# A recurrent-attention and gated-feed-forward kernel: the weights' guard made a later check, and the state-times-q products put on four 64x64 tiles

## The chip, the cores and the metric

The kernel runs on one core of a Trainium2 chip. The metric is device microseconds (us) of one execution. The core has five engines with instruction queues of their own: TensorE (PE, matmuls into PSUM; PEld is its weight load), VectorE (DVE), ScalarE (ACT), GpSimd (POOL) and SyncE (SP), which here issues every DMA. Each engine takes its instructions strictly in the order in which the program lists them.

## The reference

For each of 4 batches and 8 heads, a 48x48 state is decayed row by row with a sigmoid gate, gets the outer product of k and v added, and is read by q; the heads' outputs, side by side, are the input x of a gated feed-forward part that mixes each token with the one before it.

```python
f = 1.0 / (1.0 + np.exp(-f_logit))                 # (4, 8, 768, 48)
for t in range(S):
    state = f[:, :, t, :, None] * state + np.einsum('bhd,bhe->bhde', k[:, :, t], v[:, :, t])
    y[:, :, t] = np.einsum('bhd,bhde->bhe', q[:, :, t], state)
...
xk = mu_k * x + (1.0 - mu_k) * x_prev              # x: (4, 768, 384)
xr = mu_r * x + (1.0 - mu_r) * x_prev
k = np.maximum(xk @ w_k, 0.0)                      # w_k: 384 x 1024
v = k * k @ w_v                                    # w_v: 1024 x 384
r = 1.0 / (1.0 + np.exp(-(xr @ w_r)))              # w_r: 384 x 384
return (r * v).astype(np.float32)
```

The three weights arrive as 64-bit floats and are converted on the chip.

## The kernel before

**Attention in chunks.** Time is cut into 24 chunks `i` of 128 tokens (6 for each batch; `cs` is the chunk's place in its batch). Heads go in four pairs `j`; the head `g2` of a pair lies on partitions 0 to 47 or 64 to 111. For a chunk, `b` is the running product of the gates (a scan, L203), `bl` its last column, `ln`/`rb` give 1/b on ACT, and q and k are scaled with them (L213, L221 to L233). On PE, `SC` makes the 128x128 scores in small tiles (L274), `TR` transposes k (L259, copied out as `ktk`, L262), `ZQ` multiplies the state `z` with q (L284), `VV` adds scores times v to the same sums (L284), and `PP` makes the chunk's own contribution to the state (L315) in the PSUM tile `pp`. The masks `ma`, `mb` (L300) take the scores out of PSUM. `zs` and `z` (L247, L249) add the old state to `pp` and gate it; they come before the next chunk's `ZQ`. `y` (L330) copies the sums out of the PSUM tile `py`, negated, into `x` (pairs 0 to 2) and `stage` (pair 3). `y` of a chunk comes before `ZQ` and `VV` of the next, as there is one `py`.

**Feed-forward in units.** Three chunks make a unit `u` of 384 tokens; there are 8. When the three `y` are done, six small DMAs (`spread`, L385) move the fourth pair's rows from `stage` into the free rows of `x`. The mix (`d`, L395; `xm`, L404; `xh`, L412 or L413; `xl`, L419) makes six operands, each split into a high and a low part, because each product is made as three matmuls, high by high, high by low and low by high (`mm3`, L427). PE then runs `F` (8 groups of 9 matmuls with w_k), `R` (3 groups of 9 with w_r) and `W` (6 groups of 12 with w_v). ACT and DVE square what `F` gives (L450 to L459), POOL subtracts the high part (L465), `sg` applies the sigmoid, and `o` (L517) multiplies and is stored.

**Weights.** A 64-bit word is made into a float by `add_words`, in 18 pieces: 8 of w_k, 4 of w_r, 6 of w_v. For a piece, ACT takes the absolute value of the high half (`A`, L543), DVE clamps it from below at 2 to the power of -15 (`M`, L546, the guard for weights too small for the cheap conversion), shifts (`S`, L548), merges the low half's top bits (`T`, L551) and the sign and exponent (`X`, L554); ACT then rounds to the high part (`H`, L557) and POOL makes the low part (`L`, L561). The words of the last four pieces of w_v take turns in two buffers, `words`, which a piece leaves free when its `L` is done.

**What sets the order.** A planner (`Plan.schedule`) lists every step with a place, the engines that can do it and a cost for each, and simulates: it takes the step that can start first, and by place between equals. Its order is fixed on each engine. The constants at the file's head (`LEAD`, `PREP`, `WORDS`, `DEAR`) and the costs in `pl.add` steer it and do no work themselves. `F{u}.{f}` needs the `L` of w_k's piece f in the first unit, `R` all of w_r, a first half of `W` three pieces of w_v.

**An unusual path.** If the smallest `bl` is under a bound, a flag makes all engines run `general`, a slow exact version, at the end. The inputs here do not raise it.

Of the kernel before, what the change touches and what calls it, by code (L numbers as in the profile page):

```python
# [47 lines left out]


class Plan:  # L50
# [104 lines left out]
class Rwkv:  # L155


    def __init__(self, nc=None, tc=None):
# [17 lines left out]
    def add_attention(self, pl, i):  # L176
# [104 lines left out]
        first = [None, None]  # L281

        def ymm(g2, j, lhs, rhs, stop):
            m = nc.tensor.matmul(  # L284
                self.py[64 * g2 : 64 * g2 + lhs.shape[1], j], lhs, rhs, start=first[g2] is None, stop=stop,
                skip_group_check=True,
            )
# [36 lines left out]
        def y_out(e):  # L324

            for r in (slice(0, D), slice(64, 64 + D)) if cs == 0 else (slice(0, P),):
                for o, i_ in ((self.b("x", u)[r, :, 1 + t0 : 1 + t0 + C], self.py[r, 0:3]),
                              (self.b("stage", u)[r, t0 : t0 + C], self.py[r, 3])):
                    if e is nc.scalar:
                        e.activation(o, i_, AF.Copy, scale=-1.0)  # L330
# [50 lines left out]
    def spread(self, x, stage, j):  # L381

        for g2 in (0, 1):
            r = 64 * g2
            self.nc.sync.dma_start(x[r + 48 : r + 64, j, 1:], stage[r + 16 * j : r + 16 * j + 16, :])  # L385

    def add_mix(self, pl, u, k0, dst, alone=False):
# [46 lines left out]
        for f in range(NF):  # L434
# [36 lines left out]
        for t in range(UC):  # L471
# [343 lines left out]
```

## Time and profile before

| | |
|---|---|
| median of 3 runs | 392.2 us (391.81 to 392.32) |
| the profiled execution | 392.84 us; its span, first to last instruction, 391.1 us |
| mean granted TensorE clock | 0.977 |
| busy, share of the span | PE 87%, DVE 59%, ACT 61%, POOL 47% |
| moved by DMA | 34.17 MB, 87 GB/s over the span |

The span is 1.7 us shorter than the execution's time. Times in the trace count from the span's start. A row of the timeline gives start, length, engine, line, operation, output and inputs, count, and in brackets the idle time before it and what ended it. In a grouped row stand the count, the busy sum in us and the mean in ns, then the idle time ahead of the group. PE writes each fp32 matmul of the program as two records.

### The profile page before, as it was taken

How to read it: one execution, taken by the hardware profiler on the slowest of the kernel's cores; microseconds unless marked ns; L12 is line 12 of the kernel's file. 1: busy time of each engine (PE TensorE's matmuls, PEld its weight loads, DVE VectorE, ACT ScalarE, POOL GpSimd, SP SyncE). 2: the span in 40 equal slices, each digit the busy share in tenths (PEclk: the TensorE clock that was granted, in tenths of full speed). 3: DMA queues.
4: the chain of work that ended last, by engine and by line, in shares of the span. 5: the costliest groups of instructions: out<-in, count | busy, mean ns of one | idle time of the engine just before them, and what ended most of it. 6: DMA issues, size and time to landing. Idle time of an engine off the chain costs nothing.

```text
span 391.1 us, 8274 instructions
## 1 busy us (share of the span) xinstructions
PE 339.2 (87%) x3241; PEld 314.9 (81%) x3241; DVE 231.2 (59%) x429; ACT 237.1 (61%) x458; POOL 184.6 (47%) x212
## 2 busy tenths in 40 slices
PE   0077227699999999999999999999999999999994
PEld 0066126689898998999899989999899989999993
DVE  6989699998797588318851688049822731161001
ACT  4773348868478765747675655856584436565830
POOL 1451377764667564534574364618361613334600
PEclk9999859999999999999999999999999999999999
DMA  7999611343550243421321123032301100011001
GB/s 250 402 372 233 150 54 55 108 99 84 140 118 5 59 99 108 117 60 38 103 62 33 45 83 102 2 75 76 91 20 30 47 23 2 1 37 40 3 21 47
DMA packets 17918, 34.17 MB, mean 87 GB/s; under 512 B 2928, under 2 KB 13040, under 8 KB 17872
## 3 DMA queue, kind: packets, MB, share of 16 engines
q1 hardware_dynamic: 17872, 33.57, 30.1%
q8 instruction: 27, 0.44, 0.5%
q14 instruction: 19, 0.16, 0.1%
HBM read 27.66 MB, written 4.72 MB: 83 GB/s over the span
## 4 chain that ended last, share of the span: by engine, by line
PE 78%; DVE 9%; DMA 8%; ACT 1%; issue 1%; SPq 1%; DVEq 0%
PE pm L427 59%; PE py L284 10%; PE pss L274 5%; DMA v<-in_vt 3%; PE pm L259 2%; DMA f<-in_zt 2%; DMA x<-stage 2%; PE pp L315 2%; DVE pm L548 1%; DVE pm L551 1%; DVE pm L546 1%; DVE xm L404 1%; DVE pm L395 1%; DMA x<-in_wr 1%; DVE words L554 1%
## 5 line engine op out<-in xcount | busy, mean ns | idle before, releaser
L427 PE MATMUL pm<-xh,wk 128*128 128x384 f32 x384 | 107.5, 350 | 19.1 <-DVE words_k2h L554 13.5
L427 PE MATMUL pm<-wv,k2h 128*128 128x384 f32 x384 | 99.8, 341 | 0.4 <-DVE xm L404 0.4
L465 POOL TENSOR_TENSOR k2l<-kk,k2h 128x384 fp32r<-128x384 f32 x64 | 65.0, 1018 | 60.3 <-ACT kk L459 38.3
L427 PEld LDWEIGHTS pm<-xh,wk 128*128 128x128 f32 x384 | 71.6, 192 | 22.8 <-issue 14.1
L419 POOL TENSOR_TENSOR xl<-xm,xh 128x384 fp32r<-128x384 f32 x48 | 53.3, 1125 | 50.3 <-DVE xh L413 39.7
L427 PEld LDWEIGHTS pm<-wv,k2h 128*128 128x128 f32 x384 | 69.0, 188 | 1.8 <-issue 0.9
L427 PE MATMUL pm<-xl,wk 128*128 128x384 f32 x192 | 65.9, 343 | 0.0
L427 PE MATMUL pm<-wv,k2l 128*128 128x384 f32 x192 | 64.8, 338 | 0.0
L300 DVE TENSOR_TENSOR ss<-pss,cst_sb 128x512 f32<-128x512 f32 x48 | 30.8, 683 | 53.5 <-PE pss L274 53.3
L450 ACT ACTIVATE r<-pm 128x384 f32<-128x384 f32 x64 | 31.4, 490 | 32.2 <-PE pm L427 27.9
L274 PE MATMUL pss<-qk 64*64 64x128 f32 (+1 forms) x768 | 23.1, 258 | 22.1 <-DVE qk L225 22.1
L274 PEld LDWEIGHTS pss<-qk 64*64 64x64 f32 x768 | 19.6, 139 | 27.4 <-DVE qk L225 22.1
L427 PE MATMUL pm<-wr,xh 128*128 128x384 f32 x144 | 38.5, 349 | 0.0
L427 PEld LDWEIGHTS pm<-xl,wk 128*128 128x128 f32 x192 | 36.8, 192 | 0.0
L395 DVE TENSOR_TENSOR pm<-x 128x384 f32<-128x384 f32 x24 | 18.2, 757 | 30.9 <-DMA x<-stage 30.7
L427 PEld LDWEIGHTS pm<-wv,k2l 128*128 128x128 f32 x192 | 36.1, 188 | 0.0
L455 ACT ACTIVATE k2h<-r 128x384 fp32r<-128x384 f32 x64 | 33.6, 525 | 2.0
L517 DVE TENSOR_TENSOR o<-pm,lg 128x384 f32<-128x384 f32 x24 | 13.2, 551 | 35.7 <-PE pm L427 35.7
L221 POOL TENSOR_TENSOR qk<-qk,rb 128x256 f32<-128x256 f32 x24 | 22.5, 937 | 24.5 <-ACT rb L211 14.2
L203 DVE TENSOR_TENSOR_SCAN pm<-f,low 128x512 f32<-128x512 f32 x24 | 32.8, 1365 | 0.0
L412 ACT CAST xh<-xm 128x384 fp32r<-128x384 f32 x36 | 18.2, 514 | 20.2 <-DVE xm L404 20.0
L459 ACT ACTIVATE kk<-r 128x384 f32<-128x384 f32 x59 | 30.0, 509 | 0.1
(81 smaller groups left out, 529.2 us busy)
## 6 DMA issues: line engine op xcount, KB each, us to landing
qk<-in_qkt SPq DMA_DIRECT2D x40, 192.0 KB, 3.4
v<-in_vt SPq DMA_DIRECT2D x24, 192.0 KB, 2.5
out<-o SPq DMA_DIRECT2D x24, 192.0 KB, 1.9
words<-in_wv SPq DMA_DIRECT2D x6, 512.0 KB, 3.7
f<-in_zt SPq DMA_DIRECT2D x10, 288.0 KB, 4.9
qk<-in_qkt SPq DMA_DIRECT2D x4, 512.0 KB, 8.8
f<-in_zt SPq DMA_DIRECT2D x2, 768.0 KB, 8.4
words_k2h<-in_wk SPq DMA_DIRECT2D x4, 384.0 KB, 9.4
```

The costliest lines, as they stand in the source:

```text
L203: pl.add(f"b{i}", ga, ("V", 1.25, 1, lambda: nc.vector.tensor_tensor_scan(b().rearrange(FL), f().rearrange(FL), self.low.rearrange(FL), 1. ...
L221: e.tensor_tensor(k()[:, ::2], k()[:, ::2], rb()[:, ::2], op=ALU.mult)
L274: nc.tensor.matmul(self.pss[g2][HALF[h ^ j], j0 + j, 64 * h :], k()[HALF[g2], j0 + j, HALF[h ^ j]], q()[HALF[g2], j0 + j, 64 * h :], start ...
L284: m = nc.tensor.matmul(self.py[64 * g2 : 64 * g2 + lhs.shape[1], j], lhs, rhs, start=first[g2] is None, stop=stop, skip_group_check=True,)
L300: nc.vector.tensor_tensor(s4, p4, self.mask.unsqueeze(1).to_broadcast([P, 2, 2, C]), op=ALU.mult)
L395: pl.add(f"d{u}.{j}", pr, ("V", 0.56, 1, lambda j=j: nc.vector.tensor_tensor(pm("d", u, j)[:, :UT], x()[:, j, 1:], x()[:, j, :UT], op=ALU. ...
L419: e.tensor_tensor(lo(), xm(), hi().bitcast(F32), op=ALU.subtract)
L427: nc.tensor.matmul(ps, lhs(a, j), rhs(bb, j), start=ends[0] and i == 0, stop=ends[1] and i == len(pr) - 1)
L450: pl.add(f"r{u}.{f}", kf, ("A", 0.5, 0, lambda r=r, ps=ps: nc.scalar.activation(r(), ps(), AF.Relu)), ("V", 0.56, 0, lambda r=r, ps=ps: nc ...
L455: pl.add(f"h{u}.{f}", kf, ("A", 0.53, 0, lambda r=r, hi=hi: nc.scalar.activation(hi(), r(), AF.Square)), after=[f"r{u}.{f}"], **kw)
L459: ("A", 0.53, 0, lambda r=r, kk=kk: nc.scalar.activation(kk(), r(), AF.Square)),
L465: e.tensor_tensor(lo(), kk(), hi().bitcast(F32), op=ALU.subtract)
```

## The change

**The guard.** `A` and `M` of all 18 pieces are dropped from the usual path: `S` now reads the high half of the word itself. Instead `add_check` loads all weights a second time, in 15 pieces of up to 512 words a partition through the two `words` buffers, and DVE takes the smallest absolute value of each (`tensor_reduce`). The 15 minima join the flag at the end; if one is under 2 to the power of -15, `general` runs, which now converts the weights anew with the clamp.

**State times q.** The odd pairs' heads change sides: their sums go to the other half of the partitions, into a new tile `pz`, which is the second half of the PSUM bank of `pp`. So four neighbouring matmuls of `ZQ` use four different 64x64 corners of the array, two of `py` and two of `pz`. `y` then needs four instructions in place of two (six in place of four in a batch's first chunk), and is listed after `PP` as well as after `VV`. `spread` takes the fourth pair from the exchanged halves.

**Planner.** New constants and costs; DMA costs are counted by transfer, and a change between feed-forward and attention matmuls costs `TURN`.

```diff
-LEAD, GATE, PREP = 1.311, 0.0, 0.389
-WORDS = {"wk": (-0.353, 0.051), "wr": (-1.413, 0.009), "wv": (-0.189, 0.062)}
-HAND, DRAIN = 0.04, 0.17
-DEAR = {"V": 1.931, "A": 1.198}
+LEAD, GATE, PREP = 1.324, 0.005, 0.747
+WORDS = {"wk": (-0.342, 0.036), "wr": (-2.233, 0.009), "wv": (-0.21, 0.061)}
+HAND, DRAIN, TURN = 0.04, 0.17, 0.1
+CHECK = (2.0, 0.2)
+DEAR = {"V": 3.11, "A": 1.58}
...
-        first = [None, None]
+        first = {}
 
         def ymm(g2, j, lhs, rhs, stop):
-            m = nc.tensor.matmul(
-                self.py[64 * g2 : 64 * g2 + lhs.shape[1], j], lhs, rhs, start=first[g2] is None, stop=stop,
-                skip_group_check=True,
-            )
-            first[g2] = first[g2] or m
+
+            h = g2 ^ j % 2
+            to = (self.pz if j % 2 else self.py)[64 * h : 64 * h + lhs.shape[1], j // 2]
+            m = nc.tensor.matmul(to, lhs, rhs, start=(h, j % 2) not in first, stop=stop, skip_group_check=True)
+            first[h, j % 2] = m
+
 
         def zq():
-            for j in range(NP):
-                for g2 in (0, 1):
-                    ymm(g2, j, self.z_t[i % 2][HALF[g2], j], q()[HALF[g2], j], False)
+            for j0 in range(0, NP, 2):
+                for j in (j0, j0 + 1):
+                    for g2 in (0, 1):
+                        ymm(g2, j, self.z_t[i % 2][HALF[g2], j], q()[HALF[g2], j], False)
...
         def y_out(e):
+            x, stage = self.b("x", u)[:, :, 1 + t0 : 1 + t0 + C], self.b("stage", u)[:, t0 : t0 + C]
 
             for r in (slice(0, D), slice(64, 64 + D)) if cs == 0 else (slice(0, P),):
-                for o, i_ in ((self.b("x", u)[r, :, 1 + t0 : 1 + t0 + C], self.py[r, 0:3]),
-                              (self.b("stage", u)[r, t0 : t0 + C], self.py[r, 3])):
+                for o, i_ in ((x[r, 0:3:2], self.py[r]), (stage[r], self.pz[r, 1])):
                     if e is nc.scalar:
                         e.activation(o, i_, AF.Copy, scale=-1.0)
                     else:
                         e.tensor_scalar(o, i_, -1.0, None, op0=ALU.mult)
...
+            for r in (0, 64):
+                o, i_ = x[r : r + D, 1], self.pz[64 - r : 64 - r + D, 0]
...
         pl.add(f"y{i}", at, ("A", us, 0, lambda: y_out(nc.scalar)), ("V", us, 0, lambda: y_out(nc.vector)),
-               after=I("VV"), **({"takes" if c == 0 else "uses": [("x", u), ("stage", u)]}))
+               after=I("VV") + I("PP"), **({"takes" if c == 0 else "uses": [("x", u), ("stage", u)]}))
...
-    def spread(self, x, stage, j):
+    def spread(self, x, stage, j, turned=1):
 
         for g2 in (0, 1):
-            r = 64 * g2
-            self.nc.sync.dma_start(x[r + 48 : r + 64, j, 1:], stage[r + 16 * j : r + 16 * j + 16, :])
+            r, s = 64 * g2, 64 * (g2 ^ turned)
+            self.nc.sync.dma_start(x[r + 48 : r + 64, j, 1:], stage[s + 16 * j : s + 16 * j + 16, :])
...
-            pl.add(f"{name}A{p}", place, ("A", us(0.00104, 0.14), 0, lambda: nc.scalar.activation(
-                t(), high().bitcast(F32), AF.Abs)), after=[f"{name}{p}"], takes=[t_key], uses=[home])
             dve = us(0.00104, 0.15)
-            pl.add(f"{name}M{p}", place, ("V", dve, 0, lambda: nc.vector.tensor_scalar(
-                t(), t(), 2.0**-15, None, op0=ALU.max)), after=[f"{name}A{p}"], uses=[t_key])
-            pl.add(f"{name}S{p}", place, ("V", dve, 0, lambda: nc.vector.tensor_scalar(
-                t(I32), t(I32), 3, 0x3FFFFFFF, op0=ALU.logical_shift_left, op1=ALU.bitwise_and)),
-                after=[f"{name}M{p}"], uses=[t_key])
+            pl.add(f"{name}S{p}", place, ("V", dve, 0, shift), after=[f"{name}{p}"], takes=[t_key], uses=[home])
...
+    def add_check(self, pl):
+
+        nc = self.nc
+        pieces = [(w, slice(c, c + m)) for w, n, m in ((self.wk, KJ * DFF, 512), (self.wv, NF * DM, 512), (self.wr, KJ * DM, DM))
+                  for c in range(0, n, m)]
+        for p, (w, c) in enumerate(pieces):
+            n = c.stop - c.start
+            v = lambda p=p, n=n: self.b("words", ("c", p))[:, : 2 * n].bitcast(I32).rearrange("p (n t) -> p n t", t=2)
+            pl.add(f"c{p}", CHECK[0] + CHECK[1] * p, ("Q", n * P * 8 / 380e3, 1, lambda v=v, w=w, c=c: nc.sync.dma_start(
+                v(), w.rearrange("p a b t -> p (a b) t")[:, c])), takes=[("words", ("c", p))])
+            pl.add(f"cm{p}", CHECK[0] + CHECK[1] * p + 1, ("V", 0.00104 * n + 0.15, 0, lambda v=v, p=p: nc.vector.tensor_reduce(
+                self.least[:, p : p + 1], v()[..., 1].bitcast(F32), axis=mybir.AxisListType.X, op=ALU.min,
+                apply_absolute_value=True)), uses=[("words", ("c", p))])
+        return [f"cm{p}" for p in range(len(pieces))]
...
-    k.py = pm.tile([P, NP, C], F32, name="py")
+
+    k.py = pm.tile([P, 512], F32, name="py")[:, : 2 * C].rearrange("p (a c) -> p a c", a=2)
     k.pp = pm.tile([P, 512], F32, name="pp")
+    k.pz = k.pp[:, 256:].rearrange("p (a c) -> p a c", a=2)
+    k.least = cp.tile([P, 15], F32, name="least")
```

The planner's new order moves work in three places that the prediction speaks of, all on DVE. The first is where the first unit's `x` has been spread. `pm`, `xm` and `words` are buffers, each with its number; `L395` and `L404` are `d` and `xm`, and `L546` to `L554` are `M`, `S`, `T`, `X`. Before:

```order
L395 TENSOR_TENSOR pm_88<-x_101 128x384
L404 SCALAR_TENSOR_TENSOR xm_105<-pm_88,mu_sb,x_101 128x384
L546 TENSOR_SCALAR pm_86<-pm_86 128x384
L548 TENSOR_SCALAR pm_86<-pm_86 128x384
L551 SCALAR_TENSOR_TENSOR pm_86<-words_k2l_126,pm_86 128x384
L554 SCALAR_TENSOR_TENSOR words_k2l_126<-words_k2l_126,pm_86 128x3x128
L395 TENSOR_TENSOR pm_86<-x_101 128x384
L404 SCALAR_TENSOR_TENSOR xm_106<-pm_86,mu_sb,x_101 128x384
L546 TENSOR_SCALAR pm_89<-pm_89 128x512
L548 TENSOR_SCALAR pm_89<-pm_89 128x512
L551 SCALAR_TENSOR_TENSOR pm_89<-words_116,pm_89 128x512
```

Now (`L415` and `L424` are `d` and `xm`; `L565`, `L574`, `L577` are `S`, `T`, `X`):

```order
L415 TENSOR_TENSOR pm_90<-x_102 128x384
L424 SCALAR_TENSOR_TENSOR xm_106<-pm_90,mu_sb,x_102 128x384
L415 TENSOR_TENSOR pm_88<-x_102 128x384
L424 SCALAR_TENSOR_TENSOR xm_107<-pm_88,mu_sb,x_102 128x384
L415 TENSOR_TENSOR pm_89<-x_102 128x384
L424 SCALAR_TENSOR_TENSOR xm_108<-pm_89,mu_sb,x_102 128x384
L424 SCALAR_TENSOR_TENSOR xm_109<-pm_90,mu_sb,x_102 128x384
L424 SCALAR_TENSOR_TENSOR xm_106<-pm_88,mu_sb,x_102 128x384
L424 SCALAR_TENSOR_TENSOR xm_107<-pm_89,mu_sb,x_102 128x384
L577 SCALAR_TENSOR_TENSOR words_k2l_127<-words_k2l_127,pm_87 128x3x128
L565 TENSOR_SCALAR pm_88<-words_k2l_127 128x384
L574 SCALAR_TENSOR_TENSOR pm_88<-words_k2l_127,pm_88 128x384
```

The nine instructions of the mix's two operands stand together, ahead of what is left of w_k's pieces, and each piece has three instructions for four.

The second is at the state of the third chunk; the names in brackets are the engines whose progress an instruction waits for. Before:

```order
L247 TENSOR_TENSOR pp<-pp,z_71 128x192 [waits PE_49]
L249 TENSOR_TENSOR z_70<-pp,g 128x4x48 [waits DVE_49]
L300 TENSOR_TENSOR ss_93<-pss_81,cst_sb 128x512 [waits PE_49]
L300 TENSOR_TENSOR ss_92<-pss_82,cst_sb 128x512 [waits PE_49]
L213 TENSOR_TENSOR qk_67<-qk_67,pm_89 128x512 [waits DMAHW4_49]
```

Now (`L259` is `zs`, `L261` is `z`, `L314` the masks, `L237` a part of `k`):

```order
L259 TENSOR_TENSOR pp<-pp,z_71 128x192 [waits PE_49,Activation_49]
L314 TENSOR_TENSOR ss_94<-pss_81,cst_sb 128x512 [waits PE_49]
L314 TENSOR_TENSOR ss_93<-pss_82,cst_sb 128x512 [waits DVE_49,PE_49]
L261 TENSOR_TENSOR z_70<-pp,g 128x4x48 [waits DVE_49]
L237 SCALAR_TENSOR_TENSOR qk_67<-pm_90,qk_67 128x2x128 [waits Pool_49]
```

`zs` has a wait for ACT besides the one for PE: the ACT instruction is the last of the chunk's `y`, which reads `pz` in the bank of `pp`.

The third is at the end of the first unit's feed-forward part, where the second unit is mixed and chunk 6, the first of the third unit, gets its masks. Before:

```order
L229 SCALAR_TENSOR_TENSOR qk_66<-pm_89,qk_66 128x2x64 x2
L233 TENSOR_TENSOR pm_88<-rb_91,pm_88 128x512
L517 TENSOR_TENSOR o_114<-pm_86,lg_115 128x384
L395 TENSOR_TENSOR pm_86<-x_102 128x384
L404 SCALAR_TENSOR_TENSOR xm_107<-pm_86,mu_sb,x_102 128x384
L404 SCALAR_TENSOR_TENSOR xm_108<-pm_86,mu_sb,x_102 128x384
L225 SCALAR_TENSOR_TENSOR qk_67<-pm_88,qk_67 128x2x128
L229 SCALAR_TENSOR_TENSOR qk_67<-pm_88,qk_67 128x2x64 x2
L395 TENSOR_TENSOR pm_86<-x_102 128x384
L404 SCALAR_TENSOR_TENSOR xm_105<-pm_86,mu_sb,x_102 128x384
L517 TENSOR_TENSOR o_113<-pm_89,lg_115 128x384
L300 TENSOR_TENSOR ss_93<-pss_81,cst_sb 128x512
```

Now (`L537` is `o`):

```order
L415 TENSOR_TENSOR pm_90<-x_103 128x384
L424 SCALAR_TENSOR_TENSOR xm_108<-pm_90,mu_sb,x_103 128x384
L415 TENSOR_TENSOR pm_89<-x_103 128x384
L424 SCALAR_TENSOR_TENSOR xm_109<-pm_89,mu_sb,x_103 128x384
L424 SCALAR_TENSOR_TENSOR xm_106<-pm_90,mu_sb,x_103 128x384
L415 TENSOR_TENSOR pm_90<-x_103 128x384
L424 SCALAR_TENSOR_TENSOR xm_107<-pm_90,mu_sb,x_103 128x384
L537 TENSOR_TENSOR o_114<-pm_88,lg_116 128x384
L424 SCALAR_TENSOR_TENSOR xm_108<-pm_89,mu_sb,x_103 128x384
L314 TENSOR_TENSOR ss_94<-pss_81,cst_sb 128x512
L424 SCALAR_TENSOR_TENSOR xm_109<-pm_90,mu_sb,x_103 128x384
L314 TENSOR_TENSOR ss_93<-pss_82,cst_sb 128x512
```

All nine instructions of the second unit's mix now stand ahead of the end of chunk 6's masks, in place of five of the nine. The fifteen minima of the check stand further on, behind these rows; six of them follow each other directly ahead of the masks of chunk 11.

More of the change, by code (lines that the diff above doesn't have):

```diff
@@ L74, in schedule @@
         free = dict.fromkeys("PVAGQ", 0.0)
-        wire = 0.0
+        wire, under = 0.0, [0.0] * 8
+        last_p = "F"
         end, slot = {}, {}
@@ L114, in schedule @@
             if e == "Q":
-                done = wire = max(wire, start + 1.5) + us
-                free[e] = start + 0.06
-            else:
+                for _ in range(port):
+                    start = max(start, under[-8])
+                    wire = max(wire, start + 1.6) + us / port
+                    under.append(wire + 0.3)
+                    start += 0.45
+                done, free[e] = wire + 0.3, start
+            else:
+                if e == "P":
+                    us += TURN * ((n[0] in "FRW") != (last_p in "FRW"))
+                    last_p = n[0]
                 if port and free["G"] > start:
@@ L155 @@
 class Rwkv:
+    wk = wr = wv = None
     def __init__(self, nc=None, tc=None):
@@ L356, in add_unit @@
         else:
-            pl.add(f"f{u}", ga - 0.4 if u >= NFB else -1.5 + 0.1 * u, ("Q", 1.8, 0, load), after=gates)
+            pl.add(f"f{u}", ga - 0.4 if u >= NFB else -1.5 + 0.1 * u, ("Q", 2.07 if u < NFB else 1.55, 1 if u < NFB else 2, load), after=gates)
             if u < NFB:
@@ L365, in add_unit @@
         for j in range(KJ):
-            pl.add(f"sp{u}.{j}", u - PREP - 0.1, ("Q", 0.2, 0, lambda j=j: self.spread(x(), s(), j)), after=ys, uses=[("x", u), ("stage", u)])
+            pl.add(f"sp{u}.{j}", u - PREP - 0.1, ("Q", 0.2, 2, lambda j=j: self.spread(x(), s(), j)), after=ys, uses=[("x", u), ("stage", u)])
         if u % NU == 0:
@@ L440, in ff @@
                 mm3(ps(), lambda a, j: wk_p()[a][:, j, f * P : f * P + P], lambda a, j: sp(0)[a][:, j], range(KJ))
-            pl.add(f"F{u}.{f}", kf, ("P", 1.57, 0, ff), after=chain + [f"xl{u}.0{j}" for j in range(KJ)]
+            pl.add(f"F{u}.{f}", kf, ("P", 1.58, 0, ff), after=chain + [f"xl{u}.0{j}" for j in range(KJ)]
                    + ([] if alone else [f"wkL{f}"]),
@@ L476, in rp @@
                 mm3(ps(), lambda a, j: sp(1)[a][:, j, t * P : t * P + P], lambda a, j: wr_p()[a][:, j], range(KJ))
-            pl.add(f"R{u}.{t}", kr, ("P", 1.57, 0, rp), after=chain + [f"xl{u}.1{j}" for j in range(KJ)]
+            pl.add(f"R{u}.{t}", kr, ("P", 1.58, 0, rp), after=chain + [f"xl{u}.1{j}" for j in range(KJ)]
                    + ([] if alone else [f"wrL{p}" for p in range(4)]),
@@ L745, in general @@
             for j in range(KJ):
-                k.spread(xs[h], sg[h], j)
+                k.spread(xs[h], sg[h], j, 0)
             if h > 0:
```

101 lines of the change are left out of this document (65 added, 36 removed).

## The prediction

> **What bounds the kernel now.** I read the page's slices first: each digit is a tenth of busy time in 9.8 us.
>
> ```profile
> PE   0077227699999999999999999999999999999994
> DVE  6989699998797588318851688049822731161001
> DMA  7999611343550243421321123032301100011001
> ```
>
> PE is full from the ninth slice on; before that it mostly waits, and the DMA engines and DVE take turns at being full. I cut the span into four stages at the places where the bound changes, and asked for the busy time in each:
>
> ```profile
> core 0: us, PE busy (x) PEld busy (x) DVE busy (x) ACT busy (x) POOL busy (x), PEclk, DMA share, GB/s
> 0.00:44.60 44.60, 16.88 (x320) 13.98 (x320) 35.19 (x73) 25.27 (x47) 13.12 (x24) 1.00 0.96 295
> 44.60:79.10 34.50, 16.76 (x76) 14.61 (x80) 32.69 (x57) 22.63 (x48) 25.16 (x27) 0.76 0.27 79
> 79.10:109.20 30.10, 29.72 (x351) 27.01 (x351) 26.11 (x47) 19.25 (x37) 16.56 (x20) 0.99 0.49 116
> 109.20:385.50 276.30, 275.81 (x2506) 259.28 (x2498) 136.72 (x254) 170.00 (x330) 129.73 (x144) 1.00 0.19 53
> ```
>
> Stage A, to 44.6 us, is DMA (share 0.96). Stage B, to 79.1, is DVE (32.69 of 34.5 us). Stage C, to 109.2, and D, to 385.5, are PE. The chain of waits says the same, here with its pieces at the seams:
>
> ```profile
> 39.78 4.62 DMA x<-stage
> 44.62 0.58 DVE pm L395
> 45.23 0.62 DVE xm L404
> ...
> 71.28 0.69 DVE words L554
> ...
> 72.35 1.24 DVE pm L203
> ...
> 76.09 2.96 PE pm L427 x9
> 79.05 1.23 PE pss L274 x32
> ...
> 81.88 1.78 PE pm L427 x9
> ```
>
> The first unit's spread lands at 44.6; then DVE does mix and words in one row to about 72.4; F0.7, the last product with w_k, starts at 76.09 and ends at 79.05. From there only PE work stands in the chain, but for one step at 105.7 (below). So an instruction less on DVE counts in B, an instruction less on PE in C and D, and neither in A.
>
> **Stage A: nothing.** `A` and `M` fall away there too, but the same transfers stand ahead of the first spread on SP, and the spread is what ends the stage. Had DMA been idle at all, the new order could gain; at share 0.96 I take 0, between 0.5 less and 1.5 us more, as `y2`, which the spread waits for, has two more small instructions and now comes after PP2.
>
> **Stage B: shorter by 11 us.** The prices on DVE:
>
> ```profile
> L395 DVE TENSOR_TENSOR pm<-x 128x384 f32<-128x384 f32 x24 | 18.2, 757 | 30.9 <-DMA x<-stage 30.7
> L404 DVE SCALAR_TENSOR_TENSOR xm<-pm,mu_sb,x 128x384 f32<-128x384 f32 x48 | 28.3, 613 | 1.0
> L546 DVE TENSOR_SCALAR pm<-pm 128x384 f32<-128x384 f32 x8 | 4.5, 557 | 0.0
> L551 DVE SCALAR_TENSOR_TENSOR pm<-words,pm 128x512 int32<-128x512 int32 x6 | 4.2, 696 | 0.2
> L561 POOL TENSOR_TENSOR wk<-words_k2h,wk 128x384 fp32r<-128x384 f32 x4 | 4.1, 1019 | 14.1 <-ACT wk L557 14.1
> ```
>
> Before, from 44.62 to the last `X` of w_k, DVE does 3 `d` (0.58 in the chain), 6 `xm`, 20 instructions on w_k at 0.56 and 16 on w_v at 0.69: 1.7 + 3.7 + 11.2 + 11.0 = 27.6, and the chain shows 27.8 (to 72.4). The way of counting holds. Now there are between the same two points 3 `d`, 6 `xm`, 16 on w_k, 6 on w_v and one `zs` (0.36): 1.7 + 3.7 + 9.0 + 4.1 + 0.4 = 18.9, with `d` at its mean 0.757 it is 19.4. Part of that is the `M` dropped, more is w_v moved behind w_k. So the last `X` ends near 63.8. Behind it come the rounding on ACT (about 0.5, as a copy of 384 columns below), POOL's subtract, 1.02, and hand-offs: 65.5. POOL itself has 6 `xl` and 12 subtracts of words to do from about 46.5 on (the first `xm` ends at 45.85, then the rounding): at 1.02 each 18.4 us, somewhat more for the wide ones of w_v, so it may end as late as 67.3. F0.7 starts between the two, takes 1.78 at the usual pace and ends about 68: 11 us ahead.
>
> **Stage C: only 6.4 of the 11 us come through.** PE has, by the rows below, 110.96 - 79.05 = 31.9 us of work from there to the end of F1.0 and would be done at 68 + 31.9 - 0.9 (two `ZQ`, below) = 99. But DVE must have done what is left of w_v, the second unit's mix and chunk 6's masks. The end of this stretch before:
>
> ```profile
> 105.70 1.29 DVE ss L300 x2
> ...
> 107.03 0.91 PE py L284 x13
> ...
> 108.46 0.83 PE pss L274 x32
> 109.29 3.35 PE pm L427 x18
> ```
>
> ```profile
> L203 DVE TENSOR_TENSOR_SCAN pm<-f,low 128x512 f32<-128x512 f32 x24 | 32.8, 1365 | 0.0
> L300 DVE TENSOR_TENSOR ss<-pss,cst_sb 128x512 f32<-128x512 f32 x48 | 30.8, 683 | 53.5 <-PE pss L274 53.3
> L517 DVE TENSOR_TENSOR o<-pm,lg 128x384 f32<-128x384 f32 x24 | 13.2, 551 | 35.7 <-PE pm L427 35.7
> ```
>
> In the new order DVE has from the last `X` of w_k to the end of those masks 5 scans (6.8), 6 masks (4.1), 8 full-width `q` and `n` (5.5 at the masks' price), 4 `k` (about 1 each, 4.0), 12 instructions on w_v (8.3), 3 `d` and 6 `xm` (5.9), 3 `o` (1.7), and small ones (1.2): 37.5 us. 63.8 + 37.5 = 101.3 if it never waits. In stage C of before it was idle for 30.1 - 26.1 = 4.0 us; I take 1.0 of that, since there is more work to fill it, and keep 0 to 4. Then VV6, PP6 and SC7 follow, 2.26 us from 107.03 to 109.29: 104.6. F1.0, which stood behind them, now stands before them, so the same point before is the end of F1.0, 109.29 + 1.68 = 110.96. Gain 6.4, between 3.4 and 7.4, and up to 11.9 if PE could go ahead of DVE.
>
> **Stage D: `ZQ` halves.** PE is busy for 275.81 of 276.3 us, so each us less counts in full.
>
> ```profile
> 92.53 0.90 PE L274 MATMUL pss<-qk 64*64 64x128 f32 x32
> 93.25 1.06 PE L284 MATMUL py<-qk,z 64*64 64x128 f32 x16
> 94.24 0.62 PE L427 MATMUL pm<-wv,k2h 128*128 128x384 f32 x2
> ...
> 94.86 0.51 PE L427 MATMUL pm<-wv,k2h 128*128 128x384 f32 x2
> ...
> L284 PE MATMUL py<-qk,z 64*64 64x128 f32 x320 | 21.7, 274 | 0.2 <-ACT pm L543 0.2
> ```
>
> `SC` already runs on four 64x64 corners: 32 records in 0.72 us up to the start of `ZQ`, that is 8 steps of four, half of them half as wide, or 0.12 for a full step. `ZQ` has 16 records in two corners, 8 steps; with a record's 0.274 taken off for the last, (1.06 - 0.27) / 7 = 0.113 a step. Four steps of four instead save 4 x 0.113 = 0.45 us. Of the 20 `ZQ`, 15 lie behind chunk 6: 15 x 0.45 = 6.75, between 0 (no quads) and 15 x 0.5 = 7.5. `VV` has 128 rows and stays. A change between attention and feed-forward costs PE 0.62 - 0.51 = 0.1; the new order has two fewer: 0.2.
>
> The Trainium skill, page "PSUM — Partial Sum Buffer", section "PSUM bank collisions raise a hardware error", says that different row tiles cannot access the same bank and partitions at once; by that rule the quads need the second tile that the exchange gives them, and no run here shows quads without it.
>
> **What it adds in D, mostly hidden.** The minima: 15 on DVE. The only such instruction in the trace is small, so its price lies between that and a shift of the same width:
>
> ```profile
> L614 DVE TENSOR_REDUCE xm<-bl 128x1 f32<-128x96 f32 x1 | 0.2, 248 | 0.0
> words<-in_wv SPq DMA_DIRECT2D x6, 512.0 KB, 3.7
> 158.73 0.36 DVE L249 TENSOR_TENSOR z<-pp,g 128x192 f32<-128x192 f32 x1
> 170.45 1.29 DVE L300 TENSOR_TENSOR ss<-pss,cst_sb 128x512 f32<-128x512 f32 x2 [9.11 <-PE pss L274]
> ```
>
> I take 0.69, the nearest in width: 10 us in all, under DVE's 53.3 us of waiting for scores. The worst place is the six in a row ahead of the masks of chunk 11. There two loads fit in the buffers at a time, so the last two pairs each wait for a turnaround: 6 x 0.69 + 2 x (3.7 - 0.7) = 10.1 us, where DVE waits 9.11 today. VV11 has R2.1 ahead of it, 1.78, so I take 0.3 for it and 0.2 for the rest. If the cover were gone, the 10 us would count whole.
>
> The copies: `y` has four instructions for two.
>
> ```profile
> 97.66 0.49 ACT L330 ACTIVATE x<-py 128x384 f32<-128x384 f32 x1 [1.17 <-PE py L284]
> 98.05 0.27 ACT L330 ACTIVATE stage<-py 128x128 f32<-128x128 f32 x1
> ```
>
> 0.27 for each of the narrow ones and 0.38 (between the two rows) for the 256-wide one make 1.2 for 0.7 us. ACT has 106 us free in D. But `y` now stands between `PP` and `zs`: 1.2 + 0.36 + 0.36 + hand-offs, about 2.1 us from the end of `PP` to the next `ZQ`, where PE has a group of `F` (1.78) and `SC` (0.83) between at the tightest places, 2.6 us, and mostly `TR` too. Hidden with 0.5 to spare: 0.
>
> **Sum.** The profiled execution took 392.84 us, 0.6 over the median; 392.84 - 6.4 - 6.75 - 0.2 + 0.5 = 380.0 us.
>
> **Rivals.** *PE goes ahead of DVE in C.* For it: DVE's idle time and a mix that may land between PE's groups; against it: masks and mix are in one strict queue. The whole 11.9 us would come: 374.5.
>
> *`ZQ` doesn't shrink.* If the two tiles of one half are not written at once, its 8 steps stay: 380.0 + 6.75 = 386.8. Against it stands `SC`, which does what `ZQ` now shall.
>
> *The bank of `pp` and `pz` ties `PP`, `y` and `zs`.* For it: ACT has `r` and `h` of the groups of `F` in its queue, as wide as the copy of 0.49 above, which can use up the 0.5 us; then `y`'s 1.2 us lies bare at each of the six chunks with one group of `F` between: 380.0 + 6 x 1.2 = 387.2. By the same rule of the skill, reads of one bank by two engines may not overlap either, so the wait cannot be ordered away; before, `zs` and `y` use two banks, and no row of before shows such a wait.
>
> ```profile
> 177.34 0.57 DVE L395 TENSOR_TENSOR pm<-x 128x384 f32<-128x384 f32 x1 [5.60 <-DMA x<-stage]
> ```
>
> *The check's loads hold up the mixes; this one is slower.* SP issues in order: a load waits for a minimum, and the spreads of the third and the fourth unit stand behind five and eight loads, 6.5 rounds of two, each 3.7 + 0.7 = 4.4 us. For it: at 177 DVE still waits 5.6 us for a spread today. Against it: DVE's waits of 9 us, which cover two rounds at a time. Beyond 12.9 / 4.4 = 2.9 bare rounds the kernel is slower than before; with four, 380.0 + 17.6 = 397.6.
>
> **How the numbers follow.** The sum 0.58, PE ahead 0.14, `ZQ` unshrunk 0.08, the tied bank 0.10, the loads 0.10. The predicted time is 380.0 us. The sum's own bounds (3 us less gained in C, 1.5 more lost in A, some 2 us of stalls in D; 1 us more gained in C, 0.75 in D) give 376.5 to 386. From 373 to 389 takes in the next three cases and leaves out most of the loads and the tails, about 0.17. What a measurement here can tell from no change is 0.2%, 0.8 us: faster is below 391.4. The first four cases are faster but for 0.05 of their tails, of the loads 0.02 is faster, 0.01 the same and 0.07 slower: 0.87 faster, 0.04 the same, 0.09 slower.
>
> **What would show it.** Right: the first `d` still at 44 to 46; F0.7 ending near 68; chunk 6's masks near 102, ended by DVE's own work; `ZQ` rows of 16 records in about 0.6 us; PE without gaps over 0.5 us after 110. Wrong: F0.7 late although DVE is done (POOL or a slow clock, as at 76.09, where nine matmuls took 2.96 for 1.78); gaps on PE ended by `z` (the bank) or `xh` (the loads) in D; `ZQ` still at 1.0; or minima far from 0.69 us.

## The result, and the profile after

The changed kernel takes 379.68 us (median of 4 runs, 378.27 to 379.78) where the kernel before took 392.26 beside it. The ratio is 0.9666, 95% interval 0.9636 to 0.9697. The profiled execution is the quickest of the four, 378.27 us with a span of 376.2 us, so the stages below add up to 14.9 us less than before, 2.3 us more than the medians differ.

The slices of the page of the changed kernel:

```profile
PE   0076397898899999979999999999999999999994
DVE  8667899889986688159732686168605520161000
DMA  7999502475436753861221132022301100010001
```

From the ninth slice on PE is nearly full, as before, but the tenth and the eleventh show 8, at the end of stage C, and a dent (7) stands in the eighteenth, near 163 us. The same four stages, with the columns of the table in the prediction. They are cut at the first `d`, the end of F0.7 and the end of SC7; F1.0 lay behind the last of these cuts before (in D) and lies ahead of it now (in C), so C and D are compared in the next section's table, which cuts behind F1.0 for both:

```profile
0.00:42.50 42.50, 16.54 (x320) 13.83 (x320) 30.72 (x63) 22.49 (x47) 14.20 (x24) 1.00 0.95 310
42.50:65.20 22.70, 15.97 (x72) 13.65 (x72) 21.97 (x37) 17.18 (x38) 20.23 (x20) 0.85 0.25 74
65.20:101.10 35.90, 31.26 (x361) 28.13 (x361) 32.03 (x62) 24.46 (x50) 23.78 (x29) 0.95 0.57 157
101.10:370.60 269.50, 267.24 (x2494) 250.92 (x2490) 133.09 (x249) 179.38 (x376) 126.89 (x141) 0.99 0.27 78
```

Stage B is nearly 12 us shorter with DVE still full (21.97 of 22.7); stage C is longer, and PE now idles in it (31.26 of 35.9); in D PE has 2.3 us without work. The chain of waits at the seams:

```profile
38.35 4.06 DMA x<-stage
42.50 0.58 DVE pm L415
...
60.55 0.55 DVE words_k2l L577
...
82.23 0.83 PE pss L286 x32
83.50 2.29 PE pm L447 x12
...
95.44 1.12 PE pm L271 x4
96.56 2.39 PE pm L447 x9
...
101.14 1.76 PE pm L447 x9
```

The first `d` starts at 42.50 and the last `X` of w_k ends at 61.1. Between `SC5` and the next `W` lies `ZQ5`: 82.23 + 0.83 = 83.06 to 83.50, 0.44 us. Before, the chain showed 0.88 for it:

```profile
93.43 0.88 PE py L284 x16
```

### The profile page after: what moved, and what is told of

The parts are those of the page before. It is cut to its first block, busy times and chain, and to the rows that moved or that the text cites. A ratio compares the mean times of both kernels' runs of the same rounds, so it can differ in the third digit from the quotient of the medians.

```text
span 376.2 us, 8368 instructions
## 1 busy us (share of the span) xinstructions
PE 331.0 (88%) x3242; PEld 306.5 (81%) x3242; DVE 218.4 (58%) x409; ACT 243.5 (65%) x508; POOL 185.1 (49%) x212
## 4 chain that ended last, share of the span: by engine, by line
PE 73%; DVE 8%; DMA 8%; ACT 3%; POOL 3%; issue 2%; SPq 1%; DVEq 0%; POOLq 0%
PE pm L447 56%; PE py L299 6%; PE pss L286 5%; PE pm L271 3%; PE pp L299 3%; DMA f<-in_zt 2%; DMA words<-in_wv 2%; DMA x<-stage 2%; PE pp L329 2%; DVE pm L574 1%; DMA x<-in_wr 1%; POOL wv L584 1%; DVE pm L565 1%; DMA words<-in_wr 1%; DVE xm L424 1%
## 5 line engine op out<-in xcount | busy, mean ns | idle before, releaser
L485 POOL TENSOR_TENSOR k2l<-kk,k2h 128x384 fp32r<-128x384 f32 x64 | 66.6, 1041 | 57.8 <-ACT kk L479 47.6
L439 POOL TENSOR_TENSOR xl<-xm,xh 128x384 fp32r<-128x384 f32 x48 | 54.9, 1172 | 47.1 <-ACT xh L432 22.7
L447 PE MATMUL pm<-xl,wk 128*128 128x384 f32 x192 | 65.6, 342 | 0.0
L314 DVE TENSOR_TENSOR ss<-pss,cst_sb 128x512 f32<-128x512 f32 x48 | 30.8, 682 | 40.2 <-PE pss L286 40.1
L286 PE MATMUL pss<-qk 64*64 64x128 f32 (+1 forms) x768 | 22.7, 255 | 21.4 <-DVE qk L237 21.4
L479 ACT ACTIVATE kk<-r 128x384 f32<-128x384 f32 x64 | 32.6, 510 | 1.1 <-POOL k2l L485 0.5
L537 DVE TENSOR_TENSOR o<-pm,lg 128x384 f32<-128x384 f32 x24 | 13.2, 550 | 34.5 <-PE pm L447 34.4
L432 ACT CAST xh<-xm 128x384 fp32r<-128x384 f32 x44 | 21.6, 512 | 15.8 <-DVE xm L424 15.5
L424 DVE SCALAR_TENSOR_TENSOR xm<-pm,mu_sb,x 128x384 f32<-128x384 f32 x48 | 28.4, 615 | 3.5 <-POOL xl L439 2.5
L233 POOL TENSOR_TENSOR qk<-qk,rb 128x256 f32<-128x256 f32 x24 | 19.7, 820 | 20.6 <-ACT rb L223 13.8
```

The lines of the kernel that those rows point to most:

```text
L286: nc.tensor.matmul(self.pss[g2][HALF[h ^ j], j0 + j, 64 * h :], k()[HALF[g2], j0 + j, HALF[h ^ j]], q()[HALF[g2], j0 + j, 64 * h :], start ...
L314: nc.vector.tensor_tensor(s4, p4, self.mask.unsqueeze(1).to_broadcast([P, 2, 2, C]), op=ALU.mult)
L424: pl.add(f"xm{u}.{n}{j}", pr, ("V", 0.56, 0, lambda xm=xm, n=n, j=j: nc.vector.scalar_tensor_tensor(xm(), pm("d", u, j)[:, :UT], self.mu_s ...
L432: pl.add(f"xh{u}.{n}{j}", pr, ("A", 0.51, 0, lambda xm=xm, hi=hi: nc.scalar.copy(hi(), xm())), ("V", 0.4, 1, lambda xm=xm, hi=hi: nc.vecto ...
L439: e.tensor_tensor(lo(), xm(), hi().bitcast(F32), op=ALU.subtract)
L447: nc.tensor.matmul(ps, lhs(a, j), rhs(bb, j), start=ends[0] and i == 0, stop=ends[1] and i == len(pr) - 1)
```

## The experiments

All stages in one table, for the kernels in which order and stages can be compared. Each row is one traced execution: the start of the first `d`, the end of F0.7, the start of F1.1 (by then VV6, PP6, SC7 and F1.0 are done in most orders), the length of B and C together, and what is left of the span from there (D). The last column is the median of the timed runs.

| kernel | first `d` | F0.7 ends | F1.1 starts | B + C | D | median, us |
|---|---|---|---|---|---|---|
| before | 44.6 | 79.1 | 110.9 | 66.3 | 280.2 | 392.3 |
| before, again | 43.4 | 77.2 | 110.0 | 66.5 | 280.2 | 391.9 (one run) |
| before, one unused tile | 42.4 | 77.1 | 109.4 | 67.1 | 278.0 | 389.3 |
| before, new constants | 42.7 | 69.5 | 114.4 | 71.7 | 279.1 | 395.7 |
| before, `ZQ` only | 45.0 | 79.7 | 113.0 | 68.0 | 273.8 | 388.2 |
| changed | 42.5 | 65.2 | 101.1 | 58.6 | 275.1 | 379.7 |
| changed, old constants | 42.3 | 73.4 | 107.9 | 65.6 | 280.4 | 390.4 |
| changed, guard back | 45.6 | 75.6 | 115.9 | 70.3 | 275.2 | 395.6 |
| changed, `ZQ` back | 41.9 | 65.2 | 101.8 | 59.8 | 279.4 | 383.8 |
| changed, check small | 41.9 | 66.8 | 102.3 | 60.3 | 270.8 | 375.2 |
| changed, check late | 42.6 | 65.6 | 101.7 | 59.1 | 271.8 | 376.1 |

**What is `ZQ` worth?** The heads' sums in one tile again, order kept:

```diff
-            to = (self.pz if j % 2 else self.py)[64 * h : 64 * h + lhs.shape[1], j // 2]
+                self.py[64 * g2 : 64 * g2 + lhs.shape[1], j], lhs, rhs, start=first[g2] is None, stop=stop,
...
-            for r in (0, 64):
-                o, i_ = x[r : r + D, 1], self.pz[64 - r : 64 - r + D, 0]
```

> The changed kernel with its order kept on every engine, but the sums of all heads in one tile again, ZQ in two corners, y in two copies (four in a batch's first chunk). Theory (ZQ is worth what the sum says, and the bank of pp and pz ties nothing that matters): each of the 15 ZQ behind chunk 6 takes 0.43 us more on PE, 6.5 us, so 386 us. Rival (the bank's tie of PP, y and zs eats part of the gain): y no longer waits for that bank, some stalls vanish, and the kernel is slower by 3 us or less, 382.5.

It took 383.76 us (381.12 to 385.03), 4.1 more than the changed kernel, between the two. Adding up PE's records from F1.1 on, start to next start, settles why: all `ZQ` and `VV` take 31.5 us here, 31.2 in the kernel before, 26.2 in the changed kernel and 24.7 in it with the small or the late check. So the quads save 6.5 us from the kernel before to the last, 0.43 for each of 15 `ZQ`, as expected; the changed kernel shows less because of a stall that slowed VV11 (next), which is smaller in this variant, where `ZQ` itself is later. Nothing here needs the rival's explanation, the bank's tie.

**Is the gap ahead of VV11 the check's?** In the changed kernel DVE's rows ahead of the masks of chunk 11, and SP's:

```profile
148.95 1.27 DVE L634 TENSOR_REDUCE least<-words 128x1 f32<-128x512 f32 x2
155.81 0.69 DVE L634 TENSOR_REDUCE least<-words 128x1 f32<-128x512 f32 x1 [5.58 <-DMA words<-in_wv]
157.01 0.69 DVE L634 TENSOR_REDUCE least<-words 128x1 f32<-128x512 f32 x1 [0.52 <-DMA words<-in_wv]
160.25 0.69 DVE L634 TENSOR_REDUCE least<-words 128x1 f32<-128x512 f32 x1 [2.55 <-DMA words<-in_wv]
161.81 0.55 DVE L634 TENSOR_REDUCE least<-words 128x1 f32<-128x384 f32 x1 [0.87 <-DMA words<-in_wr]
162.28 1.27 DVE L314 TENSOR_TENSOR ss<-pss,cst_sb 128x512 f32<-128x512 f32 x2
```

```profile
148.97 0.78 SPq L368 DMA_DIRECT2D f<-in_zt  x2
149.84 7.01 SPq L632 DMA_DIRECT2D words<-in_wv  x3
157.73 4.99 SPq L632 DMA_DIRECT2D words<-in_wr  x3
```

The six minima take 13.3 us (148.95 to 162.28), the scores have been there since 158.5, and PE waits:

```profile
163.01 1.04 PE L299 MATMUL py<-ss,v 128*48 128x128 f32 x3 [2.26 <-DVE ss L314]
...
165.48 1.01 PE L447 MATMUL pm<-wr,xh 128*128 128x384 f32 x2
```

After the wait of 2.26 us VV11 lasts 2.47 us, where it usually lasts about 1. The clock that PE was granted is the reason: 0.51 (the last column but two) while VV11 ran, where it is 1.00 in the 3 us before.

```profile
163.00:165.40 2.40, 2.39 (x16) 1.72 (x16) 2.34 (x6) 0.24 (x1) 0.00 (x0) 0.51 0.79 239
```

Two variants: loads and minima cut to 8 words a partition, and minima 8 to 15 moved behind later masks.

```diff
-                v(), w.rearrange("p a b t -> p (a b) t")[:, c])), takes=[("words", ("c", p))])
+                v()[:, :8], w.rearrange("p a b t -> p (a b) t")[:, c.start : c.start + 8])), takes=[("words", ("c", p))])
```

> The changed kernel with its order kept, but each of the check's 15 loads brings 8 words a partition and each minimum is taken over those 8 alone (the rest of the weights goes unchecked). Theory (the loads' turnarounds hold up the masks of chunk 11): PE's gap of 2.26 us ahead of VV11 and VV11's slow second microsecond go, 3.3 us, so 376.4 us. Rival (the masks are late for another reason, such as zs waiting for y): the gap stays and the time is 379.5 us.

```diff
+            late = [f"mb{4 + p}"] if p >= 7 else []
...
-                apply_absolute_value=True)), uses=[("words", ("c", p))])
+                apply_absolute_value=True)), after=late, uses=[("words", ("c", p))])
```

> The changed kernel with the minima 8 to 15 tied to come after the masks of chunks 11 to 18, one for each chunk, so that none stands ahead of the masks of chunk 11 and each load has a chunk's time to land. Theory (turnarounds of the loads): as with the small check, no gap ahead of VV11, 376.4 us, with the check whole. Rival (minima cost DVE's time wherever they stand): eight gaps of 0.4 us and more, 379.5 us or slower.

The small check took 375.22 us (375.01 to 375.27), the late one 376.06 (375.62 to 376.58): the gap is gone from both, and D is 4.3 and 3.3 us shorter. So the late check, which checks every weight, beats the kernel before by 16 us and the changed one by 3.6. Its masks and VV11:

```profile
160.05 1.29 DVE L314 TENSOR_TENSOR ss<-pss,cst_sb 128x512 f32<-128x512 f32 x2 [9.57 <-PE pss L286]
```

```profile
162.13 0.42 PE L299 MATMUL py<-ss,v 128*48 128x128 f32 x4
```

The small check adds a point: its first load behind the wait, of 8 KB, still came 5 us late.

```profile
155.56 0.33 DVE L634 TENSOR_REDUCE least<-words 128x1 f32<-128x8 f32 x2 [5.18 <-DMA words<-in_wv]
```

It lies on SP behind the two loads of `f` (288 KB each), as in the changed kernel. The last three small loads, those of w_r with no `f` ahead of them, land in 1.7 us (the last column); of the three of w_v the first two are that first turnaround:

```profile
words<-in_wv SPq DMA_DIRECT2D x3, 8.0 KB, 4.2
words<-in_wr SPq DMA_DIRECT2D x3, 8.0 KB, 1.7
```

At full size the same two rows read 5.9 and 4.1. So most of the first turnaround's length is what stands ahead of it in the queue, and the bytes make the later ones long; no run moved `f` away to test this by itself.

**What is the dropped guard worth?** `A` and `M` back ahead of each `S`, order kept:

```diff
-                if clamp:
+                if True:
                     nc.scalar.activation(t(F32), high.bitcast(F32), AF.Abs)
                     nc.vector.tensor_scalar(t(F32), t(F32), 2.0**-15, None, op0=ALU.max)
```

> The changed kernel with its order kept, but A on ACT and M on DVE stand ahead of each S again; the check stays. Theory (DVE's row of words sets the end of stage B, and w_v's pieces the start of W after it): 4 M of w_k and 2 of w_v ahead of the last X of w_k, 4 x 0.48 + 2 x 0.62 = 3.2 us, 4 more of w_v behind it, 2.5 us; the stretch up to SC7 is 5 us longer, between 3 and 6: 384.7 us. Rival (the gain of stage B is the order's: mix in one piece, w_v behind w_k; a dropped M is hidden): within 1 us of the changed kernel, 380.5 at most.

395.64 us (392.37 to 397.25), 16 more than the changed kernel: neither the theory nor the rival had so much. In its trace the first `d` is 3.1 us later, B 7.2 longer, C 4.5 longer, D the same. Between the first `d` and the last `X` of w_k there are 7 `M`, not 6: 5 of w_k 0.60 apart and 2 of w_v 0.73 apart, 4.5 us; and twice DVE waits for an `A`, which ACT reaches late because roundings stand ahead of it in its queue, the second time one that itself waits for the `X` of the piece before:

```profile
52.61 0.57 DVE L563 TENSOR_SCALAR pm<-pm 128x384 f32<-128x384 f32 x1 [1.05 <-ACT pm L562]
...
61.04 0.57 DVE L563 TENSOR_SCALAR pm<-pm 128x384 f32<-128x384 f32 x1 [0.74 <-ACT pm L562]
```

Instructions and waits are 6.3 of the 7.2. So the guard does lie on the path, and the theory was low because it priced `M` alone and not `M` waiting for `A`. An order made without the guard is a bad one with it, though, so 16 us is no fair price of the guard; the next pair comes at it from the other side.

**Order or work?** The new constants on the kernel before, and the old ones on the changed kernel:

```diff
-LEAD, GATE, PREP = 1.311, 0.0, 0.389
+LEAD, GATE, PREP = 1.324, 0.005, 0.747
```

(and `WORDS` and `DEAR` with them, as in the change; the other way round for the second).

> The kernel before with the new values of LEAD, GATE, PREP, WORDS and DEAR alone, so another order of the same work. Theory (the order alone brings little; what is gained up to SC7 is A and M dropped): 392 us, between 390 and 394, F0.7 ending no earlier than 77. Rival (mix in one piece and w_v behind w_k bring the gain of stage B): F0.7 ends near 71 and the kernel takes 386 us or less.

> The changed kernel with the old values of LEAD, GATE, PREP, WORDS and DEAR, so another order of the same work. Theory (A and M dropped shorten stages A and B in either order): F0.7 ends near 67 and the kernel takes 380 us, between 378 and 382. Rival (the gain is the new order's): F0.7 near 74 and 385 us or more.

395.71 us (394.79 to 397.0) and 390.43 us (389.0 to 391.34): in neither does a theory hold whole. The new constants alone bring F0.7 forward to 69.5, so the order does shorten B by 7.6 us (26.8 against 34.4) with every `M` in place; but C then takes 44.9 us in place of 31.9: w_v, still four instructions a piece, is pushed behind, and DVE has 37.6 us of work there, where it had 26.1 before. The kernel is 2.9 us slower than the runs of before beside it. The changed kernel with the old constants has a B of 31.1 us, 3.3 shorter than before, but B + C of 65.6, hardly better, and D as long as before for all its quads (gaps of 3.45 and 1.83 us there, at 144.7 and 174.6). So in B each shortens something by itself, while the gain of B + C, 7.7 us, comes from the two together: 3 instructions for 4, in an order that lets w_k go first because w_v can afford to wait. Neither order here is quite that of the changed kernel or of the kernel before, since the planner's costs differ too.

**`ZQ` alone on the kernel before** (guard, constants and planner as before):

```diff
-            pl.add(f"ZQ{i}", at, ("P", 0.87, 0, zq), after=I("z") + I("q") + I("y", i - 1) + I("SC"))
+            pl.add(f"ZQ{i}", at, ("P", 0.48, 0, zq), after=I("z") + I("q") + I("y", i - 1) + I("SC"))
...
-    k.py = pm.tile([P, NP, C], F32, name="py")
+    k.pz = k.pp[:, 256:].rearrange("p (a c) -> p a c", a=2)
```

> The kernel before with only the exchange of the odd pairs: ZQ in four corners, pz in the bank of pp, y in four copies after PP; guard, constants and the rest of the planner as before. Theory (ZQ's saving stands by itself, 6.5 us behind chunk 6 as the accounts of the other runs show, and needs nothing of the guard's change): 385.6 us. Rival (without the guard's relief on ACT and DVE the bank's tie costs up to 0.3 us a chunk): 388 us or more.

388.19 us (386.98 to 388.54), 4.6 less than before, the rival's figure; but not for its reason. D has the 6.4 us in full (280.2 to 273.8). What is lost lies ahead of it: B and C together are 1.7 us longer, with a gap of 1.48 us ahead of `TR6`, ended by an `xm`, as this order has it wait for a `pm` bank. The bank of `pp` and `pz` ends no gap over 0.3 us behind chunk 6.

**Stage C.** In the changed kernel PE's one long gap there, and DVE's rows:

```profile
95.44 1.12 PE L271 MATMUL pm<-cst_sb,qk 128*128 128x128 f32 x4 [2.86 <-DVE o L537]
```

```profile
94.31 0.62 DVE L424 SCALAR_TENSOR_TENSOR xm<-pm,mu_sb,x 128x384 f32<-128x384 f32 x1
94.84 0.55 DVE L537 TENSOR_TENSOR o<-pm,lg 128x384 f32<-128x384 f32 x1
...
96.95 0.68 DVE L314 TENSOR_TENSOR ss<-pss,cst_sb 128x512 f32<-128x512 f32 x1
```

`TR7` waits for one of the four `pm` banks, which `o` frees, and `o` stands behind the mix, whose `d` take up others. F1.0 behind it is slow (2.39 us for 1.76): PE's granted clock is 0.50 from 95.4 to 97.6. The chain of waits names another place too, POOL's last part of w_v ahead of `W`. Both were tried on the late check: a third `words` buffer, and `d` in SBUF.

```diff
-    "o": (2, [DM]), "lg": (1, [UC, DM]), "words": (2, [1024]),
+    "o": (2, [DM]), "lg": (1, [UC, DM]), "words": (3, [1024]),
```

> The changed kernel with the late minima and a third words buffer, so that a piece of w_v is loaded while two are in work; the planner's order changes somewhat. Theory (the chain of waits is right that w_v's last pieces, through POOL, set the start of W and so stage C): SC7 is done 2 us earlier or more, 374 us. Rival (PE is full from R0.0 to the end of W0.5, and W's wait only shifted work): SC7 within 0.7 us, 375.5 to 376.5 us.

```diff
-                pm("d", u, j)[:, :UT], x()[:, j, 1:], x()[:, j, :UT], op=ALU.subtract)),
+                self.b("dd", (u, j)), x()[:, j, 1:], x()[:, j, :UT], op=ALU.subtract)),
```

> The changed kernel with the late minima, and d written to three buffers of its own in SBUF in place of three of the four pm banks of PSUM. Theory (in stage C PE waits 2.86 us ahead of TR7 for a pm bank, since o, which frees it, stands behind the second unit's mix, whose d hold the others): the gap goes, SC7 is done 1.5 to 2.5 us earlier, 374.2 us. Rival (F1.0 behind TR7 waits for the mix's low parts on POOL anyway): SC7 within 0.7 us, 375.5 us or more.

385.79 us (383.29 to 386.58) and 389.44 us (387.76 to 391.03). The planner answered both with another order, and F1.1 starts 2.5 and 3.8 us later than in the late check, not earlier. With `d` in SBUF the gap ahead of `TR7` in stage C is gone, and the next thing waits in its place, F1.0 for the mix's low parts:

```profile
96.59 0.45 PE L447 MATMUL pm<-xl,wk 128*128 128x384 f32 x1 [2.24 <-POOL xl L439]
```

That is the rival's mechanism, but as the rest of the order changed too (a gap of 3.44 us for a `pm` bank at 187.7), what C could gain stays open. The third buffer shows something else. In its order more of the check's loads, and the two loads of `f` as well, which in the late check follow the spread, are under way when the third unit is spread:

```profile
129.66 7.63 SPq L405 DMA_DIRECT2D x<-stage  x6
```

```profile
138.90 0.57 DVE L415 TENSOR_TENSOR pm<-x 128x384 f32<-128x384 f32 x1 [8.59 <-DMA x<-stage]
```

```profile
142.29 1.01 PE L447 MATMUL pm<-wv,k2h 128*128 128x384 f32 x2 [6.43 <-DVE xm L424]
```

The six small DMAs take 7.6 us to issue (3.7 in the kernel before), DVE waits for them, and PE loses 6.4 us behind the mix. How much of that is the check's loads and how much `f`, the run doesn't tell.

**The pace of PE.** From F1.1 on, all feed-forward matmuls took 216.7 us in the kernel before and 214.8 in the changed one (the long wait ahead of VV11 left out), and two changes of mode fewer explain only 0.2 of that. All variants of the changed kernel have the quicker pace too, and the two of the kernel before, with new constants and with `ZQ` alone, the slower one. So the kernel before was traced again, then given a tile that nothing uses:

> The kernel before once more, for its trace. In the traces so far a matmul of the feed-forward part follows the last after 176 ns in the kernel before and after 174 ns in the changed one and in all four variants of it, over the whole execution. If that is of the chip or the time, it is 174 here and the stage from SC7 on is some 2 us shorter than in the first trace; if it belongs to the kernel, 176 again.

```diff
+    k.least = cp.tile([P, 15], F32, name="least")
     k.flag = cp.tile([1, 1], I32, name="flag")
```

> The kernel before with one unused tile of 60 bytes a partition, allocated where the changed kernel puts its 15 minima; nothing else. In the traces, a matmul of the feed-forward part follows the last after 176 ns in the kernel before (twice), in it with only ZQ changed, and in it with the new constants; after 174 ns in the changed kernel and its variants built from it. Theory (the tile moves the buffers behind it to other addresses, which the matmuls' pace hangs on): 174 ns, 2.0 us less from SC7 on, 390.4 us. Rival (it is something else of the program): 176 ns and the time of before within 0.2%.

The second trace of before has the same pace as the first. With the unused tile it is quicker, D is 2.1 us shorter, and the kernel takes 389.27 us (388.37 to 390.94); the ratio to before is 0.9919, interval 0.9894 to 0.9943. (The medians differ by 3.3 us; the pace accounts for the 2.1 in D.) The last run moved the tile, in the late check, to behind the buffers of `F` and `R` but still ahead of those of `W`:

```diff
-    k.least = cp.tile([P, 15], F32, name="least")
...
+    k.least = cp.tile([P, 15], F32, name="least")
     k.turns = ctx.enter_context(tc.tile_pool(name="turns", bufs=1))
```

> The changed kernel with the late minima, the 15 minima's tile allocated behind all buffers of the feed-forward part in place of ahead of them; order and work the same. Theory (the addresses of the buffers set the matmuls' pace, and the tile of 60 bytes moves them to better ones): a matmul follows the last after 176 ns again, in place of 174, 2.2 us more from SC7 on: 378.3 us. Rival (the pace hangs on something else that the changed kernel has): 174 ns and 376.1 us.

375.53 us (375.32 to 375.82): no slower, since a gap of 0.53 us of the late check is missing here and `W` kept its pace. But the pace by product, ns from a matmul's start to the next one's, mean between 120 and 360 us:

| | `F` | `R` | `W` |
|---|---|---|---|
| before, both traces | 176.0 | 175.6 | 175.9 |
| before, unused tile | 174.6 | 173.5 | 173.4 |
| changed, check late | 175.3 | 173.6 | 173.4 |
| the same, tile moved | 175.8 | 176.2 | 173.4 |

`R`, whose `xh` and `xl` are now allocated ahead of the tile as in the kernel before, is slow again; `W`, whose squares `k2h` and `k2l` are allocated behind the tile in both, is not. `F`, whose `xh` and `xl` moved like those of `R`, gained only 0.7 ns in the late check and gives back 0.5. The weights are allocated ahead of the tile in every variant. So the theory's mechanism is seen in `R` and hardly in `F`; its 2.2 us reckoned with `W` too, which this place leaves alone, and `R` and `F` together lose 0.7 us.

## Why the prediction was right, and where its steps were not

Forecast 380.0 us, measured 379.68. The mechanism held in B and for `ZQ`; that the total came so close is in part luck, since the terms that missed nearly cancelled. From the profiled 392.84 us a drop of 12.8 was forecast; the profiled executions differ by 14.6 us, the medians by 12.6. Of the signs that the prediction named for being right, `ZQ`'s came true (0.44 us a chunk); the first `d` at 42.5, chunk 6's masks at 97.6 and PE's gap of 2.26 us in D did not fit.

**Stage A, "nothing": not settled.** The first `d` came 2.1 us earlier. But the same kernel before shows 44.6, 43.4 and, with an unused tile, 42.4, and the guard back costs 3.1. In that last trace the first spread lands at 43.3 and DVE, still at work on words, starts `d` at 45.6 without a wait, so in that order the transfers do not hide `A` and `M`. Whether they did in the kernel before, where `d` waits 2.82 us for the spread, isn't shown.

**Stage B, "shorter by 11 us": right.** It is 11.7 us shorter. DVE's row from the first `d` to the last `X` of w_k was priced at 18.9 to 19.4 us and took 18.6. The cause was told as the dropped `M` and the moved w_v, and the runs bear out both: another order alone shortened B by 7.6 us, the dropped `A` and `M` in the old constants' order by 3.3.

**Stage C, "only 6.4 of the 11 us come through": 7.7 of 11.7 did, by another wait.** Masks of chunk 6 were to end near 102.3 and set the stage's end; they ended at 97.6, and F1.0, late behind `TR7`'s `pm` bank and slow at a halved clock (2.39 us for 1.76), set it. DVE's row still decided, but through `o` and not through the masks. The sum of 37.5 us was of mean durations; in the trace DVE's 36.5 us hold 33.2 of work and 3.3 of waits. The rows overlap: an instruction of 0.69 us is followed 0.6 us later by the next. The overlap and the waits nearly cancelled, and the waits stayed within the bounds of 0 to 4.

**Stage D, "`ZQ` halves": right.** 0.43 us each against 0.45.

**"I take 0.3 for it": the term that failed.** The check's hold-up at chunk 11 cost 2.26 us of gap and 1.5 in the slow VV11, 3.7 in all; taking it away gave 3.6 to 4.5 us. The place was the right one and the minimum's price too (0.69), but a turnaround was priced at a `words` load's median of 3.7 us, and the first took 5.9, behind `f` on SP: 13.3 us for the six in place of 10.1. The rival of the loads is this mechanism, at the masks and not at the mixes; at a mix it is seen in the variant with three buffers, there together with loads of `f`.

**Not in the sum at all: the pace of PE,** about 2 us, by the shift in allocation that the tile of the 15 minima brought along.

So A, B and C gave 9.8 where 6.4 was forecast; D gave 5.1 (6.5 `ZQ`, 0.2 changes, 1.7 pace, less 3.3 of stalls beyond before's) where 6.45 was. The other rivals fell: PE did not get ahead of the mix in C, `ZQ` shrank, and the tied bank ended no long gap.

## What to carry to other kernels

A deferred check costs what its transfers hold up: price a turnaround with what stands ahead of it in the issuing queue, and put its consumers behind work that is waited for, one at a time. A term that shortens one stage moves its work into the next, so look at two stages together: over B and C, order and work were worth little or less than nothing alone here, and 7.7 us together. Before crediting a change with a gain spread evenly over the span, add its buffers without their use.

## What the runs showed of the hardware

An unused tile of 60 bytes a partition, which only moves the buffers allocated behind it, made the feed-forward matmuls 1.4 to 2.5 ns quicker of 176, 2.1 us in stage D. The record has the order of allocation and not the addresses, so which property of an address decides it, the runs don't tell.

After a wait of 2.26 us PE's granted clock was 0.51 for some 3 us: VV11 took 2.47 us, and the first two matmuls behind it 1.01 us for 0.51. The Trainium skill, page "TensorE: Matmul & The Clock Gate", section "What's actually happening", gives a window of about 3.4 us without work before the clock halves; here a shorter wait was enough. Nor does the length of the wait alone decide it: with the old constants one of 1.83 us was followed by a clock of 0.50, and with the guard back one of 1.95 us left it at 1.00.
